# Transposed softmax tiles: one VectorE instruction and a round trip through DRAM in place of sixteen small transposes

## The chip, the cores and the metric

One Trainium2 chip, one of its cores. The metric is the device time of one execution of the program, in microseconds (us), as the median of several runs; a profiled execution of the same program gives the trace. Engines are named as the profile names them: PE is the matmul side of TensorE and PEld its weight loads, DVE is VectorE, ACT is ScalarE, POOL is GpSimd, SP is the engine that issues the DMA transfers here.

## The reference

Attention inside chunks of 64 positions, then two feed-forward layers. Shapes: q, k, v are 8 x 8 x 576 x 64 (batch, heads, positions, head dimension), 4608 tokens in all, model width 512, inner width 2048. The first-layer weights reach the kernel as 64-bit floats.

```python
scores = scale * np.matmul(q_c, k_c.transpose(0, 1, 2, 4, 3))      # per chunk of 64
attn = np.exp(scores - scores.max(-1, keepdims=True))
attn = attn / (attn.sum(-1, keepdims=True) + 1e-09)
x = np.matmul(attn, v_c)                 # then to (tokens, heads * head_dim)
h = x @ w_in;   x = (h / (1 + np.exp(-h))) @ w_out
h = x @ w_in2;  x = (h / (1 + np.exp(-1.702 * h))) @ w_out2
```

## The kernel before

**Tiles and blocks.** Tokens are worked on in 9 blocks of 512 (4 attention tiles of 128 tokens each). The first feed-forward layer of a block runs over 16 slices of the inner width, f = 0 to 15; block and slice together are a *step*. A step is 12 matmuls that make a slice of h (`emit_h`, L419) and 12 that add an earlier slice into four accumulators (`emit_o`, L454). Each fp32 operand is split into a high and a low part, so each product is three matmuls. The attention of a block is spread over the steps of the block before it, one tile to four steps. Steps are counted here through all blocks: step 16 * block + f.

**One attention tile.** With 4m the step that is a multiple of four, the tile takes these places. At step 4m - 2 two DVE transposes (`emit_qkT`, L277) turn its loaded q and k. At step 4m - 1 TensorE makes the scores (L287), DVE takes the maximum away (L328, L332), ACT takes the exponential (L341) and DVE normalizes (`emit_norm`, L346 to L349). At step 4m `turn_e` (L378) transposes the normalized tile e into aT. At step 4m + 3 the product of aT with v runs, its 64 small matmuls laid between the 64 of the next tile's scores (`both_quads`, L287). Then ACT and DVE write the result as the next block's input (L397, L401). The tiles of the second block go another way (`emit_aT`, a TensorE transpose); `turn_e` serves the 28 tiles of the seven blocks after it, at steps 16, 20, ... 124.

**turn_e before.** DVE transposes only inside squares of 32 x 32, and a tile needs its 32-row bands at other partitions, so `turn_e` issues 16 instructions of 32 partitions x 128 elements, each reading one band of partitions and writing another.

**The order of the work is written out by hand.** Tables named first, before, softmax, middle and after hold for each step what is issued at that place, and every engine gets its instructions in that order. All DMA transfers are issued by SP, on one queue, in program order: an issue that waits holds up every one behind it.

**Other work in the same steps.** The second layer's weights are prepared meanwhile, in 16 units u = 0 to 15. For unit u, `load_u` loads 2 x 512 KB at the end of step 16 + 7u (L171, L176), `split_u` writes 1024 KB at the end of step 22 + 7u and 768 KB at the end of step 23 + 7u (both L217, after an ACT copy L212 and a DVE subtraction L214). The load of unit u + 1 stands directly behind the second write of unit u. `load_qk` (L252) and `load_v` (L265) load the next tiles' rows, and at every step with f = 1 four accumulators of 128 x 512 are copied out (L465, L467) and stored (L468).

**Buffers.** q and k turned, e, aT, the slices s and the accumulators' copies o share one pool `st` of six buffers.

Of the kernel before, what the change touches and what calls it, by code (L numbers as in the profile page):

```python
# [10 lines left out]
F32 = mybir.dt.float32  # L11
# [6 lines left out]
P = 128  # L18
# [31 lines left out]
def chunk_attention_two_ffn(  # L50
# [11 lines left out]
    nc = tc.nc  # L62
# [3 lines left out]
    HP = H // 2  # L66
# [10 lines left out]
    st_p = ctx.enter_context(tc.tile_pool(name="st", bufs=6))  # L77
# [3 lines left out]
    dram = ctx.enter_context(tc.tile_pool(name="dram", bufs=1, space=bass.MemoryType.DRAM))  # L81
# [10 lines left out]
    x1 = [dram.tile([KD, P, N], F32, name=f"x1_{i}") for i in range(NB)]  # L92
    g2 = [[dram.tile([P, N], F32, name=f"g2_{i}_{f}") for f in range(KF)] for i in range(NB)]
    w2 = [dram.tile([P, NOP * KF // 2, 2, 2 * P], F32, name=f"w2_{i}") for i in range(2)]

    w_t, raw_w = {}, {}

# [172 lines left out]
    qkT, ps_t, e_t, aT_t, x_parts = {}, {}, {}, {}, {}  # L270
# [39 lines left out]
    def of_chunk(t):  # L310
        return lambda h, c: t[CH * c:CH * c + CH, h]
# [41 lines left out]
    def emit_aT(t0, bank=None):  # L353
# [12 lines left out]
        else:  # L366
            nc.scalar.copy(out=flat, in_=bank)

    def turn_e(t0):

        e = e_t.pop(t0).rearrange("p (h c) (k n) -> p c k h n", c=2, k=2)
        aT_t[t0] = st_p.tile([P, 2, 2, HP, 32], F32, tag="st", name="aT")
        for c in range(2):
            for r in range(2):
                for j in range(2):
                    for u in range(2):
                        to, of = 64 * c + 32 * r, 64 * j + 32 * u
                        nc.vector.transpose(  # L378
                            out=aT_t[t0][to:to + 32, j, u], in_=e[of:of + 32, c, r]
                        )  # L380

    def emit_pv(t0, x, o):
        ps = at_all[:, :, BACK]
        aT = aT_t.pop(t0)
        if len(aT.shape) > 3:
            of_aT = lambda h, c: aT[CH * c:CH * c + CH, h % 2, :, h // 2]
        else:
            of_aT = of_chunk(aT)
        pending.append((ps, of_chunk(v_t.pop(t0)), of_aT))
        hi, lo = (  # L390
            x[i][:, :, o:o + P].rearrange("p h (c n) -> p h c n", c=2) for i in range(2)
        )
        x_parts[t0] = (ps.rearrange("p c (h n) -> p h c n", n=CH), hi, lo)
# [494 lines left out]
    with tc.manual_schedule():  # L888

        first, before, softmax, middle, after = {}, {}, {}, {}, {}  # L890

        def at(table, bi, f, fn, *args):
            table.setdefault((bi + f // KF, f % KF), []).append((fn, args))
# [6 lines left out]
        for bi, (layer, t0, n) in enumerate(blocks):  # L900
            if bi == 0:
                continue
            at(before, bi - 1, 0, new_x, bi)
            if layer == 0:
                for t in range(n // P):
                    ti = t0 + t * P


                    steps = tuple(
                        (bi - 1, f) for f in (  # L910
                            SECOND[t] if bi == 1 else (4 * t + i for i in (-2, -1, 1, 3))
                        )
                    )
                    if last_pv is None:
                        first_loads = [(load_qk, ti, part) for part in range(4)] + [(load_v, ti)]
                        last_qkT, last_pv = steps[0], steps[3]
                    else:
                        for part in range(4):
                            at(after, last_qkT[0], last_qkT[1] + part // 2, load_qk, ti, part)
                        at(after, *last_pv, load_v, ti)  # L920
                    last_qkT, last_pv = steps[0], steps[3]
                    at(after if bi == 1 else softmax, *steps[0], emit_qkT, ti)
                    at(before, *steps[1], emit_scores, ti)
                    at(softmax, *steps[1], emit_max, ti)
                    at(softmax, *steps[1], emit_exp, ti)
                    at(middle, *steps[1], emit_norm, ti)
                    if bi == 1:
                        at(before, *steps[2], emit_aT, ti)
                    else:
                        at(softmax, steps[1][0], steps[1][1] + 1, turn_e, ti)  # L930
                    at(first, *steps[3], lambda ti, bi, o: emit_pv(ti, x_t[bi], o), ti, bi, t * P)
                    at(softmax, *steps[3], emit_high, ti)
                    at(softmax, *steps[3], emit_low, ti)
        for u in range(KF):
            s, key = CONVERT + PACE * u, divmod(u, KF // 2)
# [257 lines left out]
        steps = [(bi, f) for bi in range(1, len(blocks)) for f in range(KF)]  # L1193
# [50 lines left out]
```

## Time and profile before

| | |
|---|---|
| median of 3 runs | 1591.16 us (1589.64 to 1591.21) |
| the profiled execution's own time | 1588.18 us |
| its span, first to last instruction | 1586.4 us |
| mean granted TensorE clock | 0.998 |
| PE busy | 1566.1 us, 99% of the span |
| DVE busy | 886.0 us, 56% |
| ACT busy | 716.4 us, 45% |
| POOL busy | 388.4 us, 24% |
| DMA | 226.19 MB, mean 143 GB/s |

The span is what the trace covers; the execution's own time has 1.8 us around it. Busy PE counts matmuls from issue to a modelled end, and they overlap, so the share says how seldom PE had none under way, not how fast it went.

### The profile page before, as it was taken

The numbers are of one execution on the slowest core, as the hardware profiler recorded it, in microseconds if no ns is written. First come the engines' busy times: TensorE is split into PE (matmuls) and PEld (weight loads), VectorE is DVE, ScalarE is ACT, GpSimd is POOL, SyncE is SP. The second block draws the span as 40 slices with busy tenths as digits, with TensorE's granted clock in tenths as the row PEclk, the third lists the DMA queues.
The fourth block names the chain that finished last, engine by engine and source line by source line (L and its number), as shares of the span: only waits on it lengthen the run. The fifth ranks groups of instructions, "written<-read, shape, count | busy, mean of one in ns | idle before, by whom it ended". The sixth has DMA issues, their size and how long they took to land.

```text
span 1586.4 us, 27152 instructions
## 1 busy us (share of the span) xinstructions
PE 1566.1 (99%) x10600; PEld 1358.4 (86%) x10600; DVE 886.0 (56%) x1462; ACT 716.4 (45%) x1038; POOL 388.4 (24%) x402
## 2 busy tenths in 40 slices
PE   8999999999999999999999999999999999999998
PEld 7778888888788888888888888888988899999998
DVE  5996576567657756666412242423423666666664
ACT  5774444453444444444323454545644333333332
POOL 1000010000000000000020030300302887777774
PEclk9999999999999999999999999999999999999999
DMA  8763454453544445353256334344388544434442
GB/s 208 229 163 93 114 131 103 113 139 102 133 113 125 108 109 139 102 137 101 103 201 220 124 142 158 121 143 141 120 290 312 182 134 130 130 123 131 131 128 76
DMA packets 279745, 226.19 MB, mean 143 GB/s; under 512 B 193601, under 2 KB 224321, under 8 KB 273985
## 3 DMA queue, kind: packets, MB, share of 16 engines
q1 hardware_dynamic: 279616, 224.47, 47.0%
q8 instruction: 83, 1.36, 0.4%
q14 instruction: 46, 0.37, 0.1%
HBM read 138.41 MB, written 85.98 MB: 141 GB/s over the span
## 4 chain that ended last, share of the span: by engine, by line
PE 85%; DVE 4%; DMA 4%; ACT 2%; SPq 2%; issue 2%; POOL 1%; DVEq 0%; ACTq 0%; POOLq 0%
PE acc L454 21%; PE h L419 21%; PE acc L572 18%; PE acc L816 11%; PE h L816 6%; PE h L572 3%; PE ps_m L816 3%; PE ps_at L287 2%; POOL sum_r L783 1%; DVE aT L378 1%; SPq L969 1%; DMA w<-split_u 1%; DMA spare<-in_moe_w_out_dram 1%; DMA t<-w 1%; DMA rows_r<-g 1%
## 5 line engine op out<-in xcount | busy, mean ns | idle before, releaser
L419 PE MATMUL h<-x,w 128*128 128x512 f32 x1728 | 420.6, 392 | 3.9 <-DVE w L155 3.9
L454 PE MATMUL acc<-g,w 128*128 128x512 f32 x1728 | 416.2, 390 | 0.0
L419 PEld LDWEIGHTS h<-x,w 128*128 128x128 f32 x1728 | 321.8, 188 | 73.4 <-PE h L1037 1.7
L454 PEld LDWEIGHTS acc<-g,w 128*128 128x128 f32 x1728 | 323.6, 188 | 67.4 <-issue 0.2
L572 PE MATMUL acc<-operand,t 128*128 128x512 f32 (+1 forms) x1200 | 274.3, 385 | 0.0
L572 PEld LDWEIGHTS acc<-operand,t 128*128 128x128 f32 x1200 | 222.3, 188 | 44.6
L430 ACT ACTIVATE s<-h 128x512 f32<-128x512 f32 x144 | 86.1, 598 | 305.9 <-PE h L419 282.9
L816 PE MATMUL acc<-t,half 128*128 128x256 f32 x1728 | 220.3, 283 | 3.5 <-ACT m L845 2.3
L199 POOL TENSOR_TENSOR raw_u<-raw_u 128x256 f32<-128x256 f32 x64 | 52.3, 839 | 692.7 <-DVE raw_u L139 514.2
L816 PEld LDWEIGHTS acc<-t,half 128*128 128x128 f32 x1728 | 212.9, 192 | 4.5 <-ACT m L845 2.5
L442 DVE TENSOR_TENSOR g<-s,g 128x512 fp32r<-128x512 f32 x144 | 99.3, 692 | 208.9 <-ACT g L432 207.7
L783 POOL TENSOR_TENSOR sum_r<-rows_r 128x256 f32<-128x256 f32 x144 | 138.7, 963 | 156.7 <-DMA rows_r<-g 67.2
L796 DVE TENSOR_TENSOR half<-rows_r,half 128x768 fp32r<-128x768 f32 x72 | 82.3, 1142 | 116.4 <-ACT half L794 116.4
L794 ACT CAST half<-rows_r 128x768 fp32r<-128x768 f32 x72 | 60.0, 833 | 190.8 <-PE acc L816 189.3
L590 DVE TENSOR_TENSOR s<-acc,u 128x512 f32<-128x512 f32 (+1 forms) x80 | 51.0, 637 | 165.8 <-PE acc L572 121.8
L378 DVE STREAM_TRANSPOSE aT<-e 32x128 f32<-32x128 f32 x448 | 135.5, 303 | 6.0
L796 DVE TENSOR_TENSOR half<-sum_r,half 128x1024 fp32r<-128x1024 f32 x72 | 111.2, 1544 | 19.6 <-ACT half L794 19.6
L816 PE MATMUL h<-t,half 128*128 128x256 f32 x864 | 115.4, 283 | 0.0
L816 PEld LDWEIGHTS h<-t,half 128*128 128x128 f32 x864 | 108.9, 192 | 0.0
L585 ACT COPY u<-acc 128x512 f32<-128x512 f32 (+1 forms) x80 | 43.5, 544 | 130.2 <-PE acc L572 129.9
L432 ACT CAST g<-s 128x512 fp32r<-128x512 f32 x144 | 89.5, 622 | 4.6
L794 ACT CAST half<-sum_r 128x1024 fp32r<-128x1024 f32 x72 | 75.3, 1046 | 28.3 <-POOL sum_r L783 28.2
(106 smaller groups left out, 1511.7 us busy)
## 6 DMA issues: line engine op xcount, KB each, us to landing
rows_r<-g SPq DMA_DIRECT2D x144, 256.0 KB, 3.0
g<-s SPq DMA_DIRECT2D x128, 256.0 KB, 2.0
t<-w SPq DMA_DIRECT2D x28, 1024.0 KB, 5.1
w<-split_u SPq DMA_DIRECT2D x16, 1024.0 KB, 4.2
w<-split_u SPq DMA_DIRECT2D x16, 768.0 KB, 4.3
x<-o SPq DMA_DIRECT2D x36, 256.0 KB, 4.1
out_dram<-o SPq DMA_DIRECT2D x36, 256.0 KB, 2.4
raw<-in_q_dram SPq DMA_DIRECT2D x256, 32.0 KB, 2.2
```

Of the source, the lines that this page charges most:

```text
L199: nc.gpsimd.tensor_tensor(out=high[:, t - T1], in0=one, in1=two, op=ALU.subtract)
L378: nc.vector.transpose(out=aT_t[t0][to:to + 32, j, u], in_=e[of:of + 32, c, r])
L419: nc.tensor.matmul(out=h[:, :n], lhsT=w[:, 0, a, c * P:(c + 1) * P], rhs=x[b][:, c, :n], start=(c == 0 and (a, b) == TERMS[0]), stop=(c == ...
L430: nc.scalar.activation(out=s[:, :n], in_=h[:, :n], func=ACTF.Silu)
L432: nc.scalar.copy(out=g[:, 0, :n], in_=s[:, :n])
L442: nc.vector.tensor_tensor(out=g[:, 1, :n], in0=s[:, :n], in1=g[:, 0, :n].bitcast(F32), op=ALU.subtract)
L454: nc.tensor.matmul(out=a[:, :n], lhsT=w[:, 1, wi, i * P:(i + 1) * P], rhs=g[:, gi, :n], start=first and (wi, gi) == TERMS[0], stop=last an ...
L572: nc.tensor.matmul(out=bank[:, :n], lhsT=of_t(0, j, WITH[o], a)[:, c * P:(c + 1) * P], rhs=x[:, b, c], start=start and (c, a, b) == terms[ ...
L783: nc.gpsimd.tensor_tensor(out=s[:, i], in0=one, in1=two, op=op)
L794: nc.scalar.copy(out=parts[0][:, to], in_=src)
L796: nc.vector.tensor_tensor(out=parts[1][:, to], in0=src, in1=parts[0][:, to].bitcast(F32), op=ALU.subtract)
L816: nc.tensor.matmul(out=bank[:, m * 2 * P:(m + 1) * 2 * P], lhsT=x[a][:, PLACE[o], m * P:(m + 1) * P], rhs=of_t(1, p, WITH[o], e), start=p ...
```

## The change

`turn_e` now issues one DVE transpose of the whole 128 x 512 tile into a new `st` buffer called turned: each 32 x 32 square is transposed where it stands. What is missing, the exchange of the squares between partition bands, is done by a new function `move_e` with five transfers on SP: one writes the 256 KB to a DRAM buffer (`te`, four of them in turn), and four read it back, one for each band of 32 partitions, 64 KB each in runs of 512 B, into the buffer that held e. `move_e` is put at the beginning of step 4m + 1, two steps ahead of the product that reads aT.

```diff
+    te = [dram.tile([P, 512], F32, name=f"te_{i}") for i in range(4)]
...
+    turned = {}
+
     def turn_e(t0):
 
-        e = e_t.pop(t0).rearrange("p (h c) (k n) -> p c k h n", c=2, k=2)
-        aT_t[t0] = st_p.tile([P, 2, 2, HP, 32], F32, tag="st", name="aT")
-        for c in range(2):
-            for r in range(2):
-                for j in range(2):
-                    for u in range(2):
-                        to, of = 64 * c + 32 * r, 64 * j + 32 * u
-                        nc.vector.transpose(
-                            out=aT_t[t0][to:to + 32, j, u], in_=e[of:of + 32, c, r]
-                        )
+        s = st_p.tile([P, 4, HP, 32], F32, tag="st", name="turned")
+        nc.vector.transpose(
+            out=s, in_=e_t[t0].rearrange("p (h c) (k n) -> p (c k) h n", c=2, k=2)
+        )
+        turned[t0] = s
+
+    def move_e(t0):
+
+        s = turned.pop(t0)
+        aT_t[t0] = (
+            e_t.pop(t0).rearrange("p a b -> p (a b)")
+            .rearrange("p (j u h n) -> p j u h n", j=2, u=2, h=HP)
+        )
+        d = te[t0 // P % len(te)]
+        nc.sync.dma_start(out=d, in_=s.rearrange("p r h n -> p (r h n)"))
+        for r in range(4):
+            nc.sync.dma_start(
+                out=aT_t[t0][32 * r:32 * r + 32].rearrange("i j u h n -> i (j u) (h n)"),
+                in_=d.rearrange("(k i) (r n) -> r i k n", k=4, r=4)[r],
+            )
...
                         at(softmax, steps[1][0], steps[1][1] + 1, turn_e, ti)
+                        at(first, *steps[2], move_e, ti)
                     at(first, *steps[3], lambda ti, bi, o: emit_pv(ti, x_t[bi], o), ti, bi, t * P)
```

## Rows read from the trace of the kernel before

**Rows 1.** The page: busy time, share of the span and instructions of each engine.

```profile
PE 1566.1 (99%) x10600; PEld 1358.4 (86%) x10600; DVE 886.0 (56%) x1462; ACT 716.4 (45%) x1038; POOL 388.4 (24%) x402
```

**Rows 2.** The chain that ended last: start, length (us), what; pieces of PE.

```profile
351.08 2.95 PE h L419 x12
374.16 2.95 PE h L419 x12
...
422.73 2.99 PE h L419 x12
...
468.92 2.95 PE h L419 x12
...
630.94 2.95 PE h L419 x12
...
700.18 2.95 PE h L419 x12
746.77 2.95 PE h L419 x12
```

**Rows 3.** Groups by line and form: count, busy us, mean ns, idle before.

```profile
L378 DVE STREAM_TRANSPOSE aT<-e 32x128 f32<-32x128 f32 x448 | 135.5, 303 | 6.0
...
L277 DVE STREAM_TRANSPOSE qkT<-raw 128x512 f32<-128x512 f32 x64 | 42.3, 691 | 7.3 <-DMA x<-o 5.4 <-issue 1.7
```

**Rows 4.** The page's DMA issues: count, KB each, median us from issue to landing.

```profile
g<-s SPq DMA_DIRECT2D x128, 256.0 KB, 2.0
...
x<-o SPq DMA_DIRECT2D x36, 256.0 KB, 4.1
...
raw<-in_q_dram SPq DMA_DIRECT2D x256, 32.0 KB, 2.2
```

**Rows 5.** DVE in order of time around step 48: start, length, what.

```profile
314.94 5.05 DVE L378 STREAM_TRANSPOSE aT<-e 32x128 f32<-32x128 f32 x16
```

**Rows 6.** SP's queue at the end of steps 74 and 102, in order of time: start, length.

```profile
463.96 4.02 SPq L252 DMA_DIRECT2D raw<-in_q_dram  x7
...
625.97 4.05 SPq L252 DMA_DIRECT2D raw<-in_q_dram  x7
```

**Rows 7.** SP's queue in order of time from step 43 to step 46.

```profile
291.46 6.97 SPq L217 DMA_DIRECT2D w<-split_u  x2
298.52 1.46 SPq L171 DMA_DIRECT2D raw_u<-in_moe_w_in_dram  x2
300.07 6.21 SPq L252 DMA_DIRECT2D raw<-in_q_dram  x8
```

**Rows 8.** ACT in the same stretch (in brackets: idle before it, and what ended it).

```profile
295.44 0.98 ACT L212 CAST split_u<-raw_u 128x512 fp32r<-128x512 f32 x2 [3.91 <-DMA w<-split_u]
```

**Rows 9.** DVE in the same stretch.

```profile
297.03 1.02 DVE L214 TENSOR_TENSOR split_u<-raw_u,split_u 128x512 fp32r<-128x512 f32 x2
```

**Rows 10.** DMA issues of 300.0-300.5, 463.9-464.4 and 625.9-626.5 us; us to landing last.

```profile
raw<-in_q_dram SPq DMA_DIRECT2D x1, 32.0 KB, 6.3
...
raw<-in_q_dram SPq DMA_DIRECT2D x1, 32.0 KB, 6.0
...
raw<-in_q_dram SPq DMA_DIRECT2D x2, 32.0 KB, 5.8
```

**Rows 11.** The same chain as in Rows 2 at steps 64 to 67.

```profile
413.86 5.86 DMA x<-o
...
421.57 1.16 PE ps_at L287 x62
```

**Rows 12.** Stretches of PE: us, busy (x instructions), granted clock, DMA share, GB/s.

```profile
24.00:30.00 6.00, 5.14 (x76) 0.72 1.11 317
418.00:422.00 4.00, 1.92 (x35) 1.00 0.47 180
```

**Rows 13.** SP's queue in order of time at step 51.

```profile
337.87 2.08 SPq L171 DMA_DIRECT2D raw_u<-in_moe_w_in_dram  x2
```

**Rows 14.** DVE in order of time at step 82.

```profile
512.27 0.71 DVE L277 STREAM_TRANSPOSE qkT<-raw 128x512 f32<-128x512 f32 x1 [1.77 <-DMA x<-o]
```

## The prediction

> **What bounds the kernel now.** I read the page first: PE is busy for 99% of the span, DVE for 56% [rows 1]. A change on DVE can therefore give back only what PE spends waiting for DVE, so the next view is the chain that ended last, along the stretch in which tiles are turned (steps 16 to 124). There the first h matmuls of a tile's turn start 23.08 us after those of the tile before (351.08 and 374.16), a beat of four steps in which PE is never short. The reader is to look for places where the beat breaks. There are four: 374.16 to 422.73 is two beats plus 2.41 us, 700.18 to 746.77 two beats plus 0.43 us [rows 2], and 0.43 us is lost twice more in the same way. All four lie where the end of step 4m also has a 1024 KB write of `split_u` (steps 36, 64, 92, 120). The lost time is 2.41 + 3 x 0.43 = 3.7 us, and no more than that can come from a shorter `turn_e`.
>
> **The change part by part.** *DVE.* 448 instructions of 303 ns, back to back 5.05 us a tile, become 28. The trace has no such instruction on e, but one of the same operation and size, 128 x 512, takes 691 ns [rows 3, 5]. DVE does 28 x 4.36 = 122 us less. On PE's path this is worth something between 0 and 3.7 us.
>
> *SP and the transfers.* `move_e` adds 28 x 5 issues. A write of 256 KB lands after 2.0 us alone and after 4.1 us where four follow each other; a band read resembles the q loads (32 partitions, 2.2 us to landing) [rows 4]; seven of those take SP 4.0 us at a time when the queue is busy [rows 6], so I take 0.5 us for each issue. So with a free queue: issue and land the write 2.3 (2.0 and a little for SP to take it up), issue four reads 2.0, land the last 2.2, in all 6.5 us after the turn. The product starts 1.16 us before the first h matmuls of its step (421.57 and 422.73 [rows 2, 11]). In an ordinary tile the turn begins at 314.94 [rows 5] and would end at 315.6; its product is due at 351.08 - 23.08 - 1.16 = 326.84. 11.2 us against 6.5: hidden, with 4.7 us to spare. The reads wait for the write, and while they wait SP issues nothing; behind them stand the stores of o at steps with f = 1 and the next tiles' loads. The loads have over 10 us in hand, the stores have none (below).
>
> *The three tiles at steps 44, 72 and 100.* Here the last things SP is given before `move_e` are the 768 KB write of one unit and the 2 x 512 KB loads of the next. In the old kernel SP issues that write with those at the end of step 44, loads at 298.52, and the transfer issued next, at 300.07, is a q load [rows 7]. A q load lands after 2.2 us as a rule [rows 4], but this one needed 6.3, its counterparts at steps 72 and 100 6.0 and 5.8 [rows 10]: what is issued behind the loads waits until they are through. `move_e`'s write takes exactly this place. It comes a little sooner than the q load did, because DVE reaches the second subtraction sooner; but not by the 4.36 us of the turn, since that subtraction also waits for ACT, which waits until 295.44 for the first write of `split_u` to land [rows 8], and that one is issued before the turn. The first half of the copy is ready at about 296.1 where DVE began at 297.03 [rows 9]: 0.9 us sooner. So the write lands at 300.07 + 6.3 - 0.9, plus 0.5 for its larger size, = 306.0 (between nothing, since alone a 256 KB write lands no later than a q load [rows 4], and 0.8, 256 KB at the 317 GB/s of a busy stretch [rows 12]); the last read is issued 1.5 later and lands 2.2 after that, at 309.7. The product is due one beat before 326.84, at 303.76. PE waits 6.0 us. At step 72 the first h matmuls start at 468.92, the product 1.16 earlier, at 467.76; the q load issued at 463.96 [rows 6] plus 6.0 - 0.9 + 0.5 + 3.7 gives 473.3: 5.5 us. At step 100 due is 630.94 - 1.16 = 629.78 [rows 2], and 625.97 [rows 6] + 5.8 + 3.3 = 635.1: 5.3 us. Together 16.8 us. The bounds: with the write landing 2.0 us after an issue at 299.2 (298.52 + 1.46 and a little, less 0.9) as if nothing lay ahead, the last read lands at 304.95, 1.2 us late, 3.6 us for three; with another 2 us on each, 23 us. I take the value from the nearest rows, those of the q loads behind the same loads.
>
> The page "DMA: Bandwidth & Descriptors" of the Trainium skill, section "Queues, rings and completion order", says that descriptors of a ring are taken in order but that a later transfer may complete before an earlier one; by that rule the write could land early, which is the rival "hidden", 1591 in place of 1610. The q loads of [rows 10] did not do so.
>
> *The clock after such a wait.* With 2.1 us idle between 418 and 422 the granted clock stayed 1.00; at the start of the kernel, in a stretch in which PE ran out of work repeatedly, it averaged 0.72 over 6 us [rows 12], 6 x 0.28 = 1.7 us of full speed lost. For an idle PE of 5 to 6 us no row exists; bounds 0 and 1.7 us a tile, I take 1.2 (the wait is longer than all that kept the clock): 3.6 us in all. The skill's page "TensorE: Matmul & The Clock Gate", section "Part 1: The HAM clock gate (the "warmup" mystery)", has an idle TensorE put back to 1.2 GHz until it has been busy again; by it the term would be nearer its upper end, 5.1 us, and the sum 1.5 us higher; the trace has it both ways [rows 12].
>
> *The four tiles where the beat breaks now.* At steps 36, 92 and 120 everything on DVE after the turn comes some 3 us sooner until the second `split_u`, bound by the landing of the first write. The 0.43 us goes away: -1.3. `move_e`'s write stands behind 1024 KB there; I get its reads landing about 1 us before the product. At step 64 the four stores of o follow too. There the chain runs through the store of the first o (issued at 413.86, landing 5.86 later), whose buffer the turned k takes, to the scores at 421.57 [rows 11]. The chain now begins 3 us sooner, but the o stores stand behind a write and four reads, 6.5 us of SP's time with a free queue. Between 2.4 us won and 2.4 more lost the two nearly cancel; I take -0.5.
>
> *The four tiles with loads one step earlier* (steps 24, 52, 80, 108). At step 52 the loads are issued from 337.87 to 339.95 [rows 13]. A write behind them lands 6.3 later, at 346.2, and the last read at 349.9; the product is due at 351.08 - 1.16 = 349.92 [rows 2]. Nothing, by a hair. At step 80 the four stores of o stand behind the reads, 2.6 us later than now; the transpose of k that waits for the first of them already starts late at 512.27 [rows 14], where the scores are due at 514.0 (two beats after 468.92, less 1.16): 1.0 us is left. I take +0.9, out of 0 to 2.
>
> *The sum.* 16.8 + 3.6 - 1.3 - 0.5 + 0.9 = 19.5 us on the profiled execution's own time of 1588.2: 1607.7. That execution lies 3.0 us under the median of the runs, so for the median 1591.2 + 19.5 = 1610.7; I say 1610.
>
> **The rivals.** *Hidden.* The move's write passes the loads or shares the engines evenly with them. For it: with a free queue 6.5 us of 11.2 are needed. Against: [rows 10]. Even then the three tiles are 1.2 us late each, +3.6, against 3.7 given back: 1591, no change.
> *Faster.* The price is the read behind the write: if the last read lands within 4.5 us of the write's issue at 299.2 (303.76 less that), nothing is late even at step 44 and the shorter turn shows: 1591.2 - 3.7 = 1587.5. It decides at that point alone; the cheapest rows give 5.7.
> *Milder.* The write lands after 4.1 us as stores in a row do, the three tiles lose 3.3 us each, and the clock holds: 9.9 - 1.8 + 0.9, 1600.
> *Worse.* Six of the tiles that I find on time by up to 1 us (36, 92, 120, 24, 52, 108) lose 1.5 us each and the clock 1.7 after each long wait: 16.8 + 5.1 + 9.0 + 0.9 - 0.5 = 31, 1622.
>
> **How the numbers follow.** Forecast 0.55, milder 0.15, worse 0.15, hidden 0.09, faster 0.06. About 0.2% (3.2 us) is what a measurement of this kernel can tell from no change. The first three are slower: 0.85; hidden is the same: 0.09; faster 0.06. The range runs from 1597, a little under milder, to 1622, at worse; it leaves out hidden, faster and the upper part of worse.
>
> **What would show it.** Right: DVE busy near 764 us with 28 transposes of about 0.7 us on e; PE's waits headed by the product of step 47, 75 and 103, waiting for DMA some 5 to 6 us each; SP's queue held between the write and the first read for 6 us there and about 2 us in ordinary tiles; the beat of 23.08 us unbroken elsewhere; a granted clock under 1.00 in the microseconds behind the three waits. Wrong: a write that lands 2 to 3 us after its issue behind the loads, or the second `split_u` subtraction of steps 44, 72 and 100 done several microseconds sooner than now, so that the move comes well before 299; then the waits shrink towards nothing and only 3.7 us are left to win.

## The result, and the profile after

The changed kernel takes 1610.3 us (median of 4 runs, 1609.67 to 1611.43) against 1590.4 us (the kernel before, with a fourth run): ratio 1.0126, 95% interval 1.0112 to 1.014. That is 20 us slower, with DVE 110 us less busy. The profiled execution took 1610.9 us, 22.8 us more than the profiled one of before. In the experiments below, one run of 4045.6 us (the wait filled with matmuls) and one of 3077.5 us (the o stores issued by ACT) took far longer than the others of their kernel and are left out of medians and ratios.

The page of the changed kernel, busy time of each engine, answers to [rows 1]:

```profile
PE 1575.3 (98%) x10600; PEld 1366.4 (85%) x10600; DVE 775.9 (48%) x1042; ACT 716.9 (45%) x1038; POOL 389.9 (24%) x402
```

In the groups by line, the new transpose, which was priced by the one of 691 ns in [rows 3] (count, busy us, mean ns, idle before):

```profile
L376 DVE STREAM_TRANSPOSE turned<-e 128x512 f32<-128x512 f32 x28 | 19.8, 706 | 0.3
```

So `turn_e` did become as cheap as hoped. What PE waits for (us in all, times, longest) has a new head that before had no counterpart:

```profile
PE ps_at L289 <- DMA e<-te: 13.7, 6, 4.4
```

Six waits, two in each of three products. The writes land, as a rule, quickly, and some do not (DMA to landing, min/median/max, from the instructions of the tile `turned`):

```profile
DMA to landing us min/median/max: 2.0/2.1/7.1
```

SP's queue at steps 43 to 46, which answers to [rows 7], shows one of the slow ones:

```profile
290.58 6.05 SPq L219 DMA_DIRECT2D w<-split_u  x2
296.72 1.45 SPq L173 DMA_DIRECT2D raw_u<-in_moe_w_in_dram  x2
298.22 0.70 SPq L389 DMA_DIRECT2D te<-turned  x1
304.79 1.75 SPq L391 DMA_DIRECT2D e<-te  x4
```

The write is issued at 298.22, straight behind the weights' loads, and the first read follows at 304.79: 6.6 us, in which SP issues nothing else. The turn itself had ended at about 291.2; for the 7 us until 298.22 the write stands behind the 768 KB write, which waits for its own data, and the loads. On PE's weight loads (in brackets the idle time and what ended it) the product begins in two parts, since its first matmuls need only the first two of the four bands:

```profile
307.30 0.14 PEld L289 LDWEIGHTS ps_at<-e,v 64*64 64x64 f32 x1 [4.77 <-DMA e<-te]
...
308.52 0.18 PEld L289 LDWEIGHTS ps_at<-e,v 64*64 64x64 f32 x1 [0.89 <-DMA e<-te]
```

On PE itself the idle times are 4.38 us (its line at 307.33 stands below) and 0.73:

```profile
308.55 0.34 PE L289 MATMUL ps_at<-e,v 64*64 64x64 f32 x1 [0.73 <-DMA e<-te]
```

The stretches of PE around it (us, busy, granted clock, DMA share, GB/s) show that the loss does not stop there:

```profile
303.00:307.30 4.30, 0.00 (x0) 1.00 0.36 115
307.30:308.50 1.20, 0.49 (x8) 0.53 0.50 97
308.50:310.00 1.50, 1.45 (x53) 0.50 0.46 70
310.00:312.00 2.00, 2.00 (x17) 0.50 0.27 43
312.00:314.00 2.00, 2.00 (x6) 0.50 0.62 133
314.00:316.00 2.00, 2.00 (x10) 0.95 0.64 103
```

Once PE has work again it does it at the lower of its two clocks (0.50, 1.2 GHz) until shortly after 314. The busy time of each stretch times what its clock lacks of 1.00 is 0.2 + 0.7 + 1.0 + 1.0 + 0.1 = 3.0 us. The page "TensorE: Matmul & The Clock Gate" of the Trainium skill, "Part 1: The HAM clock gate (the "warmup" mystery)", has an idle TensorE set back to 1.2 GHz until it has been busy for a time; this trace agrees, 0.50 in these stretches.

The beat of 23.08 us [rows 2] can be followed in the first matmul of each product, on PE in order of time:

```profile
279.81 0.27 PE L289 MATMUL ps_at<-e,v 64*64 64x64 f32 x1
307.33 0.30 PE L289 MATMUL ps_at<-e,v 64*64 64x64 f32 x1 [4.38 <-DMA e<-te]
334.10 0.27 PE L289 MATMUL ps_at<-e,v 64*64 64x64 f32 x1
...
426.42 0.32 PE L289 MATMUL ps_at<-e,v 64*64 64x64 f32 x2
451.00 0.27 PE L289 MATMUL ps_at<-e,v 64*64 64x64 f32 x1
...
527.64 0.33 PE L289 MATMUL ps_at<-e,v 64*64 64x64 f32 x2
552.19 0.27 PE L289 MATMUL ps_at<-e,v 64*64 64x64 f32 x1
```

The tile of step 44 takes 27.52 and the next 26.77: 4.44 + 3.69 = 8.1 us lost, 4.38 + 0.73 = 5.1 of it idle and 3.0 the clock. Those of steps 72 and 100 lose 7.4 and 7.5 in the same way, together 23.0: 13.7 us of idle PE (the six waits) and 9.3 of work at the lower clock. The break at step 64 has shrunk from 2.44 to 24.58 - 23.08 = 1.5, the three of 0.44 us are gone, and step 80 has a new one of 24.55 - 23.08 = 1.5. All other beats are 23.08. The sum, 23.0 - 0.9 - 1.3 + 1.5 = 22.3, is the profiled executions' difference but for half a microsecond.

### The profile page after: what moved, and what is told of

Same layout as the page of the kernel before. It is cut to its first block, busy times and chain, and to the rows that moved or that the text cites. A ratio compares the mean times of both kernels' runs of the same rounds, so it can differ in the third digit from the quotient of the medians.

```text
span 1609.2 us, 27049 instructions
## 1 busy us (share of the span) xinstructions
PE 1575.3 (98%) x10600; PEld 1366.4 (85%) x10600; DVE 775.9 (48%) x1042; ACT 716.9 (45%) x1038; POOL 389.9 (24%) x402
## 4 chain that ended last, share of the span: by engine, by line
PE 86%; DMA 5%; DVE 3%; ACT 2%; issue 2%; SPq 1%; POOL 1%; DVEq 0%; ACTq 0%; POOLq 0%
PE h L433 21%; PE acc L468 21%; PE acc L586 18%; PE acc L830 12%; PE h L830 6%; PE h L586 3%; PE ps_m L830 3%; PE ps_at L289 2%; DMA te<-turned 2%; POOL sum_r L797 1%; DMA w<-split_u 1%; DMA rows_r<-g 1%; DVE split_u L216 0%; DMA g<-s 0%; PE h L1052 0%
## 5 line engine op out<-in xcount | busy, mean ns | idle before, releaser
L433 PE MATMUL h<-x,w 128*128 128x512 f32 x1728 | 425.7, 396 | 3.7 <-DVE w L157 3.7
L433 PEld LDWEIGHTS h<-x,w 128*128 128x128 f32 x1728 | 326.1, 190 | 74.5 <-PE h L1052 1.6
L612 ACT ACTIVATE s<-s 128x512 f32<-128x512 f32 (+1 forms) x120 | 70.9, 591 | 30.8 <-DVE s L604 30.4
```

What stands on the lines that cost most here:

```text
L433: nc.tensor.matmul(out=h[:, :n], lhsT=w[:, 0, a, c * P:(c + 1) * P], rhs=x[b][:, c, :n], start=(c == 0 and (a, b) == TERMS[0]), stop=(c == ...
L612: nc.scalar.activation(out=s[:, :n], in_=src[:, :n], func=ACTF.Silu, scale=act_scale[1])
```

## The experiments

Each is an edit of the changed kernel. Theory: the write of `move_e` stands, at steps 44, 72 and 100, behind other transfers in SP's queue. Rivals: the round trip is too long for two steps; the added traffic; the load on the DMA engines, whoever issues.

**The move directly behind the turn.** With this the five transfers stand ahead of whatever the end of step 4m gives SP.

```diff
-                        at(first, *steps[2], move_e, ti)
+                        at(softmax, steps[1][0], steps[1][1] + 1, move_e, ti)
```

> The five transfers are issued directly behind the turn, at step 4m instead of the beginning of step 4m + 1, so that they stand ahead of the write and the loads of the weights at the end of step 4m. Theory (the changed kernel lost its time because the write to DRAM stood behind 768 KB and 2 x 512 KB in SP's queue at steps 44, 72 and 100): the write lands within 2 to 4 us, the product of steps 47, 75 and 103 waits for nothing, the granted clock stays at 1.00; what stays is step 80, 1.5 us, against 1.3 to 3.7 us given back by the shorter turn: 1587 to 1591 us. Rival (the round trip is too long for a lead of two steps, or the added traffic is the price): the product goes on waiting, 1605 to 1611 us.

Measured: 1587.97 us, ratio to the kernel before 0.9979 (0.997 to 0.9988): faster than both. PE waits for `te` nowhere. SP's queue at step 44, and lower down at step 80:

```profile
290.89 0.35 SPq L389 DMA_DIRECT2D te<-turned  x1
294.83 1.74 SPq L391 DMA_DIRECT2D e<-te  x4
296.68 0.38 SPq L219 DMA_DIRECT2D w<-split_u  x1
297.15 1.49 SPq L173 DMA_DIRECT2D raw_u<-in_moe_w_in_dram  x2
...
498.23 1.34 SPq L178 DMA_DIRECT2D raw_u<-in_moe_w_out_dram  x2
499.66 0.46 SPq L389 DMA_DIRECT2D te<-turned  x1
507.02 1.75 SPq L391 DMA_DIRECT2D e<-te  x4
508.87 1.86 SPq L482 DMA_DIRECT2D x<-o  x4
```

The same round trip, the same bytes: the reads now follow the write after 3.9 us (it still has the 1024 KB write of step 43 ahead of it) and are issued 10 us sooner than in the changed kernel. At step 80 the loads stand ahead in this version too (they belong to the end of step 79), the write takes 7.3 us, and one product comes late, 535.01 instead of 533.37:

```profile
510.29 0.32 PE L289 MATMUL ps_at<-e,v 64*64 64x64 f32 x2
535.01 0.27 PE L289 MATMUL ps_at<-e,v 64*64 64x64 f32 x1
```

**Only the loads behind the move.** The 768 KB write stays ahead, the 2 x 512 KB don't.

```diff
-            at(after, 0, s, load_u, *key)
+            at(first, 0, s + 1, load_u, *key)
```

> Only the loads of the next unit's weights are moved behind the five transfers (to the beginning of the next step); the 768 KB write stays ahead of them. Theory: what stands ahead in the queue is the price, so a smaller amount costs less: the write to DRAM lands at about 301.2 instead of 304.8, the reads about 2 us after the product is due instead of 5.6; 0.5 to 2 us for each of three tiles, and no fall of the clock, since the wait is short: 1590 to 1597 us. Rival (the loads ahead are not the cause): 1608 to 1612 us.

Measured: 1591.1 us, ratio 0.9998 (0.9989 to 1.0007), no change. SP's queue at step 44:

```profile
296.66 0.42 SPq L389 DMA_DIRECT2D te<-turned  x1
300.65 1.74 SPq L391 DMA_DIRECT2D e<-te  x4
302.49 0.94 SPq L173 DMA_DIRECT2D raw_u<-in_moe_w_in_dram  x2
```

4.0 us for the write where it was 6.6, and at PE the two waits of this product, 4.77 and 0.89 before:

```profile
303.04 0.13 PEld L289 LDWEIGHTS ps_at<-e,v 64*64 64x64 f32 x1 [0.51 <-DMA e<-te]
304.03 0.13 PEld L289 LDWEIGHTS ps_at<-e,v 64*64 64x64 f32 x1 [0.76 <-DMA e<-te]
```

With 2.1 us free, 4 us behind 768 KB and 6.6 us behind that and 1 MB of loads, the wait follows what is queued ahead. It does so only roughly: the write of step 64, behind 1024 KB, takes 6.0 us in the changed kernel and here, and 4.2 us in the version with the wait filled, with the same order in the queue. Three short waits leave the clock alone (1.00). The 20 us are gone, but the gain doesn't show: 1.1, 0.5 and 0.7 us are still lost at the three tiles and 1.4 and 1.5 at steps 64 and 80, together 5.2, against the 3.7 that the shorter turn gives back.

**Only the turn.** No transfers; the product reads the squares where they stand, so the exchange between partition bands is left out.

```diff
-        turned[t0] = s
+        e_t.pop(t0)
+        aT_t[t0] = s.rearrange("p (j u) h n -> p j u h n", j=2)
...
-                        at(first, *steps[2], move_e, ti)
```

> Only the first half of the change: the one transpose a tile, and no transfers; the exchange of the 32 x 32 squares between partitions is left out, and the product reads the squares where they stand. Theory: this is all that the change can give, 3.7 us, every break of the beat of 23.08 us in the stretch of the turned tiles: 1586 to 1588 us. Rival (DVE was not what PE waited for at these places, or the buffer that is held longer takes the gain): 1589.5 to 1591.5 us.

Measured: 1585.6 us, ratio 0.9967 (0.9954 to 0.9979), that is 5.2 us or between 3.3 and 7.3; the 3.7 expected lies inside, though the median is 0.4 us under the range of 1586 to 1588. PE over the stretch of the turned tiles (us, busy, granted clock):

```profile
120.00:765.00 645.00, 645.00 (x4476) 1.00 0.44 115
```

PE is never short in it and the beat never breaks: this is all that a cheaper turn can give.

**Only the transfers.** The 16 transposes stay and are what the product reads; the write and four reads (of 32 KB, half the size) are issued at `move_e`'s place into a buffer that nobody reads.

```diff
+    back_t = const.tile([P, 2, HP * 32], F32, name="back")
...
-                out=aT_t[t0][32 * r:32 * r + 32].rearrange("i j u h n -> i (j u) (h n)"),
-                in_=d.rearrange("(k i) (r n) -> r i k n", k=4, r=4)[r],
+                out=back_t[32 * r:32 * r + 32],
+                in_=d.rearrange("(k i) (r n) -> r i k n", k=4, r=4)[r][:, :2],
```

> Only the second half: the 16 transposes a tile stay, the product reads their result, and the write and four reads (half as large, 32 KB each) are issued at the same place for nobody. Theory: SP is held as long at steps 44, 72 and 100, but nobody on PE's path waits for it; only the stores of o at steps 65 and 81 come later, by some 4 and 1.5 us: 1591 to 1598 us. Rival (the added traffic, or what is queued behind the waiting reads, is the price): 1605 to 1612 us.

Measured: 1596.5 us, ratio 1.0033 (1.0021 to 1.0045). The traffic (with reads of half the size) and SP's held queue cost about 5 us, not 20. The writes of steps 44, 72 and 100 are as slow as in the changed kernel (6.8, 6.1 and 5.7 us to the first read), and the beat there is 23.08 all the same, since no product waits for them. About half of what the tiles lose in the profiled execution (4.0 of 8.0 us) is one place, step 64, where the o stores wait behind the reads; the rest is up to 1.0 us each at steps 32, 36, 48, 80 and 112. PE's longest wait and the two products around it:

```profile
PE ps_at L289 <- DVE qkT L279: 7.4, 6, 4.6
```

```profile
420.48 0.32 PE L289 MATMUL ps_at<-aT,v 64*64 64x64 f32 x2
450.02 0.27 PE L289 MATMUL ps_at<-aT,v 64*64 64x64 f32 x1
```

29.54 against 25.52 before (a beat and the 2.4 us that [rows 2] show there): 4.0 us more. Of the 6.5 us over the beat 4.6 are the wait; behind it the clock is 0.50 until 429, some 1.7 us.

**The wait filled with matmuls.** To part the wait from the clock, PE gets work of no use in front of the three products.

```diff
+        def fill_wait(bi, f):
+            ps, w, x = bank(), w_t[0, f], x_t[bi]
+            for _ in range(24):
+                nc.tensor.matmul(
+                    out=ps, lhsT=w[:, 0, 0, :P], rhs=x[0][:, 0, :N], start=True, stop=True
+                )
+
+        for g in (47, 75, 103):
+            at(first, *divmod(g, KF), fill_wait, *divmod(g, KF))
```

> The changed kernel, with 24 extra matmuls of 128 x 512 (5.4 us at the full clock) into a free bank in front of the product at steps 47, 75 and 103, so that TensorE works while it waits; nothing of the result is changed. Theory (of the 22 us lost about 9 are the half clock after each wait, not the wait): the transfers land as late as before, the granted clock stays at 1.00 there, and 2.8 us are saved for each of the three tiles: 1600 to 1603 us. Rival (all of the loss is the wait for the transfers): 1609 to 1612 us, or more where the extra work outlasts the wait.

Measured: 1602.1 us, ratio 1.0068 (1.005 to 1.0087). The tile of step 44 on PE, and the stretch of the wait (us, busy of PE, PEld, DVE, ACT and POOL, granted clock, DMA share, GB/s):

```profile
280.58 0.27 PE L289 MATMUL ps_at<-e,v 64*64 64x64 f32 x1
309.10 0.27 PE L289 MATMUL ps_at<-e,v 64*64 64x64 f32 x1
332.18 0.27 PE L289 MATMUL ps_at<-e,v 64*64 64x64 f32 x1
```

```profile
303.00:309.00 6.00, 6.00 (x28) 4.78 (x26) 0.72 (x2) 0.00 (x0) 0.00 (x0) 1.00 0.47 152
```

28.52 and then 23.08: 5.44 us lost, which is the 24 matmuls, and nothing after. So 8.1 - 5.4 = 2.7 us of this tile were the clock, or 3.0, since the matmuls take 0.3 longer than the idle time that they fill. At steps 72 and 100, too, 5.44 us are lost, where it was 7.4 and 7.5; there the matmuls outlast the 4.3 us of idle time by 1.1. The three tiles give back 6.7 us. That the median lies 8.2 under the changed kernel's and inside the expected range is partly luck: the breaks at steps 64 and 80 shrank too, from 1.5 us each to nothing and 0.2, where their writes landed after 4.2 and 5.9 us in place of 6.0 and 7.2, and so the o stores behind them came sooner; why, these runs don't show.

**Issued by POOL.** `nc.sync` becomes `nc.gpsimd` in the five transfers.

> The five transfers are issued by POOL at the same place in the program instead of by SP; SP keeps the weights' write and loads. Theory (SP's order is the price, not the DMA engines' load nor the two steps): POOL has nothing ahead of them, so the write is issued right behind the turn, lands within 2 to 4 us, and the stores of o at steps 65 and 81 no longer stand behind the reads; no wait for the transfers anywhere and the beat unbroken: 1585 to 1588 us. Rival (the load on the DMA engines or the round trip is the price): waits at the same three products, 1600 to 1611 us.

Measured: 1599.3 us, ratio 1.0055 (1.0041 to 1.0069): the wait is smaller than in the changed kernel but not gone; neither expectation was right. PE's waits, POOL at the tile of step 48, and the four reads of step 44 (KB each, us to landing):

```profile
PE ps_at L289 <- DMA e<-te: 9.4, 9, 2.1
```

```profile
319.09 3.16 POOL L201 TENSOR_TENSOR raw_u<-raw_u 128x256 f32<-128x256 f32 x4 [19.25 <-DVE raw_u L141]
322.19 0.58 POOL L389 DMA_DIRECT2D te<-turned  x1
```

```profile
e<-te POOLq DMA_DIRECT2D x4, 64.0 KB, 5.8
```

Two things replace SP's queue. POOL has work of its own ahead of the write (the differences for the weights, 3.2 us, behind which the write is issued at 322.19): 7.4 of the 9.4 us of waits are at the tiles of steps 28, 48, 56, 76, 84 and 104, all of which have this work in front. And a transfer from another engine's queue is still slowed by what SP has under way: the reads of step 44, issued beside SP's 768 KB and loads, needed 5.8 us to land (6.0 at step 100, 3.6 at step 72) instead of the 2.4 that is POOL's median. That costs the tiles of steps 44 and 100 the other 2.0 us, and that of step 72 nothing. The page "DMA: Bandwidth & Descriptors" of the Trainium skill, section "Issuing engines are not separate DMA queues", says that transfers of all issuing engines run on the same 16 DMA engines and interleave; these 5.8 us agree. With the write issued as soon as the turn is done, the load on the engines costs 2 us at the three tiles where the changed kernel loses 23. POOL's transfers are counted on a queue of another kind (`software_dynamic`, SP's on `hardware_dynamic`), which this comparison can't set apart.

**Without DRAM.** Sixteen transfers of 16 KB, directly behind the turn, from buffer to buffer.

```diff
...
         for r in range(4):
+            for k in range(4):
+                nc.sync.dma_start(
+                    out=aT_t[t0][32 * r:32 * r + 32, k // 2, k % 2], in_=s[32 * k:32 * k + 32, r]
+                )
...
```

> The transfers are issued directly behind the turn, and go from buffer to buffer on the chip without DRAM: 16 transfers of 16 KB (one for each pair of bands) that wait only for the turn, in place of a write and four reads that wait for it. Theory (it is the place in SP's queue that counts, and what SP is held for): SP is busy for about 8 us a tile with issuing but waits for no landing, so much the same as the early version with DRAM: 1586 to 1591 us, with the stores of o at step 81 late again. Rival (the round trip through DRAM is itself the price): clearly below the early version, 1584 to 1586 us.

Measured: 1684.8 us, ratio 1.0591 (1.0575 to 1.0606). A clear miss of both expectations. SP's queue at the first tile, and DVE there:

```profile
129.13 10.99 SPq L390 DMA_DIRECT2D e<-turned  x16
140.16 1.13 SPq L173 DMA_DIRECT2D raw_u<-in_moe_w_in_dram  x2
141.41 3.00 SPq L480 DMA_DIRECT2D x<-o  x4
```

```profile
141.65 0.71 DVE L279 STREAM_TRANSPOSE qkT<-raw 128x512 f32<-128x512 f32 x1 [4.62 <-DMA e<-turned]
147.18 0.71 DVE L279 STREAM_TRANSPOSE qkT<-raw 128x512 f32<-128x512 f32 x1 [4.82 <-DMA x<-o]
```

The issues alone hold SP for 10 to 11.5 us a tile, in every tile, nearly half a beat, where I had 8; the turning of q then waits for the buffer `turned`, the turning of k for the o stores that stand behind. The transfers themselves land 1.8 us (median) after their issue, so the number of issues, and not the landing, is what SP is held for. PE waits 31.9 us for `qkT` and 24.0 us for these transfers, 56 of the 98 us that the profiled execution is longer; its mean granted clock is 0.976 against 0.998. How the rest divides between the clock and other waits stays open. Whether DRAM has a price of its own this run can't say.

**The o stores issued by ACT**, on top of the early move, and the early move again on the same chip.

```diff
-                nc.sync.dma_start(out=x1[bi][i], in_=o[:, :n])
+                nc.scalar.dma_start(out=x1[bi][i], in_=o[:, :n])
```

> The early version (transfers directly behind the turn, on SP) with the stores of the accumulators' copies o issued by ACT instead of SP, so that they no longer stand behind the four reads. Theory (the one break of the beat left in the early version, 1.6 us at step 80, is these stores behind the reads): the beat is unbroken in the whole stretch, 1.6 us less than the early version: ratio to the kernel before 0.9965 to 0.9975, against 0.998. Rival (that break comes from the loads on the DMA engines, whoever issues the stores, or ACT loses as much by issuing): 0.9975 to 0.999.

> The early version once more on the same chip, to be compared with the version whose o stores are issued by ACT: 0.997 to 0.999 of the kernel before, with one break of about 1.6 us at step 80.

Measured: 1585.8 us, ratio 0.9975 (0.9964 to 0.9986), and 1587.6 us, 0.9981 (0.9972 to 0.999). The one break left is gone but for 0.07 us (534.14 - 510.99 = 23.15, against 24.54 for the early move on this chip), so it was the stores behind the reads:

```profile
510.99 0.27 PE L289 MATMUL ps_at<-e,v 64*64 64x64 f32 x1
534.14 0.27 PE L289 MATMUL ps_at<-e,v 64*64 64x64 f32 x1
```

The two intervals of the ratio overlap, and 0.9975 is where the expected range and the rival's meet. The runs themselves lie apart: seven average 1586.0 us and the eleven of the early move 1587.6, and the 1.6 us between them are the size of the break.

## Why the prediction was right

*The place of the loss: right.* Three products, of the tiles of steps 44, 72 and 100, wait for the transfers, because the write stands behind 768 KB and the loads. Moving the move ahead, or only the loads behind it, takes the loss away; the transfers without a reader cost 5 us and nothing at these three tiles; the turn alone gains. The rivals of a round trip that is too long for two steps and of the added traffic are out: the same round trip one place earlier beats the kernel before. The load on the DMA engines is not quite out: from POOL's queue two of the three tiles still waited, 2.0 us in all.

*The size of the wait: too large by 3.1 us.* 16.8 us were worked out, 13.7 measured (5.1, 4.3 and 4.3). The moment of the write's issue was right to 0.1 us. It came at 298.22, not 299.2, but the whole execution lies 0.9 us earlier there: the product before is at 279.81 (above), and before the change it was at

```profile
280.68 0.27 PE L287 MATMUL ps_at<-aT,v 64*64 64x64 f32 x1
```

So the product of step 44's tile was due at 302.89, and its write was issued 4.7 us ahead of that, worked out as 4.6. The landing behind the loads was nearly right (6.6 us, worked out as 6.3 + 0.5); the last bands came 5.7 us after the product was due, worked out as 5.9, and at steps 72 and 100 4.8 and 4.7, worked out as 5.5 and 5.3. What the prediction left out is that the first matmuls of the product need only two of the four bands: eight matmuls (of 64, half of them the next tile's scores) run before the last read lands, so that PE is idle for less than the lateness.

*The clock: far too small.* 1.2 us a tile were taken, 1.7 the upper bound; 3.0 to 3.2 came. The bound came from a stretch at the start of the kernel in which PE had gaps of at most 1.25 us and the clock was low for little over 3 us; behind the three waits it was low for about 6 us of work. This is the term that was mis-sized: 3.6 us in the sum, 9.3 measured. What sets its length stays open: behind the 4.6 us wait of the version with only the transfers it was 3.6 us.

*The gain, the borderline tiles and the o stores: right.* The three breaks of 0.44 us vanish (-1.3 both ways); step 64 gives 0.9 back, where 0.5 was taken, and step 80 costs 1.5, where 0.9 was taken. None of the six tiles that were found on time by a hair was late.

*The sum.* 19.5 us were forecast on the profiled executions, 22.8 came; the medians differ by 19.9. That 1610.0 met 1610.3 so closely is luck: the errors of the wait (3.1 us too much) and of the clock (5.7 too little) cancel in part, and so does the step from profiled execution to median: that of before lay 2.2 us under its median, that of after 0.6 over. DVE's saving was worked out as 122 us with the gaps between the 16 instructions counted as busy; the transposes give 135.5 - 19.8 = 115.7, DVE's other instructions took 5.6 us longer, and 110 came.

## What to carry to other kernels

A transfer that must be read back is priced by what its queue holds ahead of it at that moment, so look up for each place, not on average, which bulk transfers end the step before. Where an issue waits for a landing, count everything behind it on that engine as held, and put it where nothing bulky is ahead or where nothing urgent is behind. A long wait of TensorE was paid twice here: 13.7 us idle, and 9.3 more at the lower clock behind it.

## What the runs showed that I had not expected

- After 3.6 to 4.6 us without work PE ran at half its clock, for 3.6 us (only the transfers) to about 6 us of work (the changed kernel); after 0.65 us (the loads behind the move) and after 2.1 us [rows 12] it didn't.
- SP needed 0.6 to 0.7 us for each of the 16 transfers of 16 KB, but 0.42 us for one of 64 KB in runs of 512 B (1.75 us for four).
- Reads of 64 KB on POOL's queue landed after 5.8 us beside SP's bulk transfers, and after 2.4 us as a rule.
